# Window attention, forward and backward: the attention products recast as 64x64 tiles

## The chip, the cores and the metric

The kernel runs on one core of a Trainium2 chip. The metric is the device time of one execution in microseconds; the median of seven runs before the change is 1990.57 us (1983.88 to 1993.39). The profile is of one further execution.

## The reference, cut to what matters

An image of 256x256 positions with 384 channels is cut into 1024 windows of 8x8 positions (64 tokens). Each window gets single-head attention without bias; the kernel must return the output and, for a given gradient of the output, the gradients of `x`, `wqkv` and `wo`.

```python
xw = windows of x                     # (1024, 64, 384)
q, k, v = split(xw @ wqkv)            # 384 -> 3 * 384
p = softmax((q @ k.T) * 384 ** -0.5)
out_0 = unwindow((p @ v) @ wo)
out_1, out_2, out_3 = vjp(grad_out)   # of x, wqkv, wo
```

All tensors are bf16.

## The kernel before

**Algebra.** The weights are multiplied together once at the start. With A = Wq Wk^T (scaled), B = Wv Wo and their transposes, a window with tokens x and output gradient g needs: y = x A and z = g B^T (`project`), scores y x^T and dP = z x^T (`scores`), u = x B and v = x A^T (`uv`), softmax P and its gradient dS (`soft`), and then in `attend` three kinds of result: the output o = P u; the gradient d = P^T z + dS^T y + dS v; and U = dS x and W = P^T g, out of which the weight gradients are summed over all windows (`gf_group`, GF_acc). The left factor of a matmul is its stationary operand and is taken transposed, so P and dS as they stand serve P^T z, P^T g and dS^T y, and the turned ones (`PS`) serve P u, dS v and dS x.

**Tiling.** Two windows (128 tokens) are a tile, four tiles a quad; there are 128 quads. Tokens lie on the 128 partitions, window 0 of a tile on the lower half (LO) and window 1 on the upper (HI). z and y leave `project` with channels on the partitions, as columns (window, token) of one tile `yz` whose four slots are ordered z, y, y, z, and must be turned to tokens on the partitions (`tok`) before `attend` uses them.

**Stages.** `step(c, b, a, ahead)` works on three quads at once: `project` for quad a, `scores`, `soft` and `uv` for quad b, `attend` for quad c, in two pairs of tiles. A quad is loaded (`load`) three steps ahead. `load_turn`, ahead of the step, turns a later quad's dq and xq (dT, xT). In a step the order on TensorE is: `scores`; `uv` (8 banks); `project` kind 0 (z, reads dT); one block of the filler; `attend` of tiles 0 and 1; `project` kind 1 (y, reads xT); another block of the filler; `attend` of tiles 2 and 3. The filler is `gf_group`: 12 matmuls over three earlier quads into one bank, which DVE then adds to GF_acc.

**Order.** The order is written out by hand for all five engines (`manual_schedule`); each engine works its list through in order and waits on semaphores. All products go to one ring of eight PSUM banks, given out in turn: the ninth bank asked for is the first again, and waits until its last reader is done. ACT and DVE copy the banks out: ACT z, y, u, v, o, d and one U, DVE the other U and W and GF_acc. SyncE's queue issues, in this order, dT, xT, PS, four xq loads and tok; GpSimd's the dq loads and the stores.

**Shapes on TensorE.** `split` makes `product` issue a 128x128 product as two of 128 rows and 64 columns. It is set between the two `attend`s, so that `project` kind 1 and the filler there have the 128x64 shape that `attend` begins and ends with (`token_part`). `token_part` (lines 261 to 264) is P^T z + dS^T y of a window in one product of 128 rows: `ps` holds P of one window and dS of it on the two halves, so that the token rows z and y add up over the 128 partitions. It needs dS on the half opposite to P (line 224), and tok with z and y of a window on the two halves. The four products of a window pair in `both` (64x64) go to the four quarters of the array: two straight ones (LO to LO, HI to HI) and two crossed ones (LO to HI, HI to LO). The crossed results land on the other half, so that o and d are each kept in two banks, and a bank holds halves of both tiles; they are stored in one store of 128 rows and two of 64 (lines 292 to 297).

Of the kernel before, what the change touches and what calls it, by code (L numbers as in the profile page):

```python
# [14 lines left out]
P = 128  # L15
# [7 lines left out]
def kernel(  # L23
# [120 lines left out]
    ALL = False  # L144
    split = [ALL]

    def product(out, lhsT, rhs, start, stop):
        if split[0]:
            for h in (LO, HI):
                nc.tensor.matmul(out[h], lhsT=lhsT[:, h], rhs=rhs, start=start, stop=stop)  # L150
        else:
            nc.tensor.matmul(out, lhsT=lhsT, rhs=rhs, start=start, stop=stop)  # L152
# [3 lines left out]
    def project(st, kind, mo):  # L156
        if kind == 0 and mo == 0:
            st["yz"] = qp.tile([P, CK, QUAD, 4, WT], BF16, tag="yz", name="yz")
# [10 lines left out]

    def to_tokens(st):  # L170
        st["tok"] = tok = qp.tile([P, CK, QUAD, 2, P], BF16, tag="tok", name="tok", bufs=3)
        nc.sync.dma_start_transpose(out=tok[:].rearrange("p m t b k -> p (m t b) k"),
                                    in_=st["yz"][:].rearrange("p m t s k -> p (m t s k)"))
# [13 lines left out]
    def soft(st, step):  # L187
# [31 lines left out]
        else:  # L219
# [3 lines left out]
            for w, h, o in ((0, LO, HI), (1, HI, LO)):  # L223
                nc.vector.tensor_tensor(out=ps[o, :, w, :], in0=st["pr"][h, :, :], in1=pd[h, :, :], op=ALU.subtract)

    def uv(st, t, part):
        if t == 0 and part == 0:
            for n in ("uq", "vq"):
                st[n] = qp.tile([P, QUAD, C], BF16, tag=n, name=n)
        wgt, dst, cp = ((B_sb, st["uq"], ENG[EV["u"][t]]), (AT_sb, st["vq"], ENG[EV["v"][t]]))[part]  # L230
        pj = ring.tile([P, C], F32, tag="r")
        for m in range(CK):
            product(pj[:], st["xT"][:, t, m, :], wgt[:, m, :], m == 0, m == CK - 1)
        cp(out=dst[:, t, :], in_=pj[:])  # L234
# [6 lines left out]
    def turned(st, n, t, h):  # L241
        if n in ("PT", "ST"):
            return st["PS"][h, t, int((n == "ST") == (h == LO)), :]
        return st[n][h, t, :]

    def attend(st, pair):
# [7 lines left out]
        def both(straight, crossed, t, outer, **flags):  # L254
            for h, o, (dst, lhs, rhs), fl in ((LO, LO, straight, {}), (LO, HI, crossed, flags), (HI, LO, crossed, flags),
                                              (HI, HI, straight, {})):
                at = dst if dst is not crossed[0] else dst[outer if h == LO else 1 - outer]
                nc.tensor.matmul(at[o, :], lhsT=turned(st, lhs, t, h), rhs=st[rhs][h, t, :],  # L258
                                 **{"start": True, "stop": True, **fl})

        def token_part(t, pd, outer, **flags):
            for w, o in ((0, HI), (1, LO)):
                nc.tensor.matmul(pd[outer if w == 0 else 1 - outer][o, :], lhsT=st["ps"][:, t, w, :],  # L263
                                 rhs=st["tok"][:, :, t, w, :], **flags)

        def keep(name, dst, src):
            for outer in (0, 1):
                sb = ob.tile([P, C], BF16, tag=name, name=name)
                nc.scalar.copy(out=sb[:], in_=src[outer][:])  # L269
                stores.append((dst, sb, outer))  # L270

        t0, t1 = pair
        stores = []
        pu = [bank("pu")]
        po = [bank("po") for outer in (0, 1)]
        pd = [bank("pd") for outer in (0, 1)]
        token_part(t0, pd, 1, start=True, stop=False)
        both((pu[0], "ST", "xq"), (po, "PT", "uq"), t0, 1)
# [47 lines left out]
    def step(c, b, a, ahead):  # L326
# [30 lines left out]
        for mo in range(CK):  # L357
            A(project, 1, mo)
# [120 lines left out]
```

## Time and profile before

| | |
|---|---|
| median of 7 runs | 1990.57 us |
| profiled execution | 1990.69 us, its span 1988.9 us |
| TensorE busy | 1967.2 us, 19487 matmuls |
| VectorE (DVE) busy | 1260.2 us |
| ScalarE (ACT) busy | 1461.2 us |
| GpSimd (POOL) busy | 1122.7 us, DMA issues |
| DMA | 423.66 MB, mean 213 GB/s |
| granted TensorE clock | 1.000 |
| issue to landing, median | tok 8.2, xT 6.7, dT 6.6, PS 4.8 us |

A group line of the profile names the source line, engine, operation, the tiles written and read, the shape and count; behind the first bar busy time and mean duration (ns), behind the second the idle time of the engine just before it and what ended it. In the order of time a line has the start, the duration (both us), the engine and how many instructions are merged. Matmul durations overlap: what one costs is the distance from its start to the next one's. "128*64" is the part of the array that a product uses, rows by columns. SPq is SyncE's queue.

### The profile page before, as it was taken

The page shows a single profiled execution, that of the slowest core. Times are in us where ns is not written, and L with a number is a line of the kernel's source. Part 1 is how long each engine was busy: PE and PEld are TensorE (multiplying, and loading weights), DVE is VectorE, ACT ScalarE, POOL GpSimd, SP SyncE. Part 2 cuts the span into 40 slices and gives each one's busy share as a digit, 9 for nine tenths or more (in the row PEclk, how much of TensorE's full clock was granted, in tenths as well). Part 3 has the DMA queues.
Part 4 walks back from the last instruction along what each step waited for, and adds up shares of the span by engine and source line. Part 5 has one row for each costly group of instructions (what it writes and reads, how often), then busy time and mean ns, then how long its engine had stood idle before and what let it go on. Part 6 is the DMA issues. An engine that isn't in the chain of part 4 may idle for free.

```text
span 1988.9 us, 52531 instructions
## 1 busy us (share of the span) xinstructions
PE 1967.2 (99%) x19487; PEld 1125.2 (57%) x19487; DVE 1260.2 (63%) x2860; ACT 1461.2 (73%) x3357; POOL 1122.7 (56%) x2054
## 2 busy tenths in 40 slices
PE   9999999999999999999999999999999999999999
PEld 5555555555555555555555555555555555555555
DVE  5656666666666666666666666666666666666666
ACT  7867777777777777777777777777777777777774
POOL 3655555555555556555555565555555655655553
PEclk9999999999999999999999999999999999999999
DMA  8999999999999999999999999999999999999994
GB/s 178 222 205 219 208 227 208 219 219 214 219 216 219 223 206 228 216 208 217 219 218 214 222 210 221 213 221 218 226 216 219 213 216 213 222 221 220 210 210 108
DMA packets 1036032, 423.66 MB, mean 213 GB/s; under 512 B 918016, under 2 KB 1011200, under 8 KB 1035776
## 3 DMA queue, kind: packets, MB, share of 16 engines
q1 hardware_dynamic: 935984, 267.85, 81.3%
q0 software_dynamic: 98304, 151.39, 30.8%
q8 instruction: 152, 2.49, 0.5%
q10 hardware_dynamic: 1488, 1.08, 0.2%
q14 instruction: 104, 0.85, 0.2%
HBM read 101.84 MB, written 101.84 MB: 102 GB/s over the span
## 4 chain that ended last, share of the span: by engine, by line
PE 82%; DMA 4%; ACT 1%; DVE 0%; SPq 0%; issue 0%; ACTq 0%
PE pj L152 30%; PE pg L152 11%; PE pj L150 11%; PE pg L150 11%; PE pd L263 6%; PE pu L258 5%; PE sd L152 4%; PE pw L258 4%; DMA dT<-dq 3%; DMA PS<-ps 1%; PE pd L258 0%; PE pe L377 0%; ACT uq L234 0%; ACT vq L234 0%; SPq L134 0%
## 5 line engine op out<-in xcount | busy, mean ns | idle before, releaser
L297 POOL DMA_DIRECT2D out_dram<-o x256 | 139.1, 543 | 682.6 <-ACT o L269 663.4
L313 DVE TENSOR_TENSOR GF_acc<-pg,GF_acc 128x384 f32<-128x384 f32 x258 | 143.9, 558 | 527.3 <-PE pg L150 372.3
L269 ACT CAST o<-po 128x384 bf16<-128x384 f32 x512 | 221.8, 487 | 248.0 <-issue 247.7
L152 PEld LDWEIGHTS <-xT 128*128 128x128 bf16 x3072 | 291.9, 98 | 182.3
L152 PE MATMUL pj<-B_sb,xT 128*128 128x384 bf16 x1536 | 333.4, 326 | 0.0
L152 PE MATMUL pj<-AT_sb,xT 128*128 128x384 bf16 x1536 | 333.3, 326 | 0.0
L127 POOL DMA_DIRECT2D dq<-in_grad_out_dram x512 | 274.2, 546 | 82.7 <-DMA out_dram<-o 42.9
L152 PE MATMUL pj<-dT,BT_sb 128*128 128x512 bf16 x1152 | 269.7, 379 | 10.5 <-DMA dT<-dq 7.5
L150 PE MATMUL pj<-xT,A_sb 128*64 128x512 bf16 x2304 | 270.2, 379 | 0.0
L234 ACT CAST uq<-pj 128x384 bf16<-128x384 f32 x512 | 247.6, 484 | 29.3 <-PE pj L152 25.2
L234 ACT CAST vq<-pj 128x384 bf16<-128x384 f32 x512 | 249.8, 488 | 2.1
L269 ACT CAST d<-pd 128x384 bf16<-128x384 f32 x512 | 227.1, 510 | 0.2 <-ACT o L269 0.2
L152 PEld LDWEIGHTS <-xq 128*128 128x128 bf16 x1572 | 153.6, 98 | 114.7 <-issue 0.3
L150 PEld LDWEIGHTS <-xq 128*64 128x64 bf16 x3000 | 167.8, 110 | 89.0
L212 ACT COPY ps<-Pb 64x256 bf16<-64x256 bf16 x256 | 103.3, 403 | 149.7 <-DVE Pb L209 148.2
L168 ACT CAST yz<-pj 128x512 bf16<-128x512 f32 x384 | 208.0, 655 | 0.3 <-PE pj L150 0.2
L166 ACT CAST yz<-pj 128x512 bf16<-128x512 f32 x384 | 206.3, 639 | 0.6 <-PE pj L152 0.2
L152 PEld LDWEIGHTS <-BT_sb 128*128 128x128 bf16 x1152 | 111.4, 98 | 136.5 <-DMA dT<-dq 16.5
L150 PEld LDWEIGHTS <-A_sb 128*64 128x64 bf16 x2304 | 131.5, 110 | 97.5 <-DVE D L218 0.4
L152 PE MATMUL pg<-Uq,xq 128*128 128x384 bf16 x1032 | 181.6, 326 | 0.0
L258 PE MATMUL pu<-xq,PS 64*64 64x384 bf16 x1024 | 175.6, 335 | 2.5 <-DMA PS<-ps 2.0
L263 PE MATMUL pd<-tok,ps 128*64 128x384 bf16 x1024 | 177.6, 344 | 0.0
(87 smaller groups left out, 3388.0 us busy)
## 6 DMA issues: line engine op xcount, KB each, us to landing
xq<-in_x_dram SPq DMA_DIRECT2D x512, 96.0 KB, 4.1
dq<-in_grad_out_dram POOLq DMA_DIRECT2D x512, 96.0 KB, 4.0
out_dram<-o POOLq DMA_DIRECT2D x256, 96.0 KB, 4.3
out_dram<-o POOLq DMA_DIRECT2D x512, 48.0 KB, 4.4
out_dram<-d POOLq DMA_DIRECT2D x256, 96.0 KB, 4.6
out_dram<-d POOLq DMA_DIRECT2D x512, 48.0 KB, 4.6
tok<-yz SPq DMA_TRANSPOSE x128, 8.2
PS<-ps SPq DMA_TRANSPOSE x128, 4.8
```

What stands on the lines that cost most here:

```text
L127: nc.gpsimd.dma_start(out=dq[:, t, :], in_=windows(grad_out, st, 2 * t))
L150: nc.tensor.matmul(out[h], lhsT=lhsT[:, h], rhs=rhs, start=start, stop=stop)
L152: nc.tensor.matmul(out, lhsT=lhsT, rhs=rhs, start=start, stop=stop)
L166: ENG[EV["z"][mo]](out=yz[:, mo, :, 0:4:3, :], in_=pj[:])
L168: ENG[EV["y"][mo]](out=yz[:, mo, :, 1:3, :], in_=pj[:])
L212: nc.scalar.copy(out=ps[h, :, w, :], in_=Pb[h, :, :])
L234: cp(out=dst[:, t, :], in_=pj[:])
L258: nc.tensor.matmul(at[o, :], lhsT=turned(st, lhs, t, h), rhs=st[rhs][h, t, :], **{"start": True, "stop": True, **fl})
L263: nc.tensor.matmul(pd[outer if w == 0 else 1 - outer][o, :], lhsT=st["ps"][:, t, w, :], rhs=st["tok"][:, :, t, w, :], **flags)
L269: nc.scalar.copy(out=sb[:], in_=src[outer][:])
L297: nc.gpsimd.dma_start(out=windows(dst, st, 2 * t0 + 1), in_=sb[:])
L313: nc.vector.tensor_tensor(out=GF_acc[:, f, ma, :], in0=pw[:], in1=GF_acc[:, f, ma, :], op=ALU.add)
```

## The change

- z and y are no longer turned out of `yz`: DVE first copies them apart into a new tile `zy` (`gather`, once for z after the first `attend`, once for y after `project` kind 1), and `tok` is turned out of `zy`, z and y in two blocks, window 0 on LO and window 1 on HI. `yz` has one buffer instead of two.
- DVE also keeps dS on the half where it is computed (`dS`); the crossed copy in `ps` stays, for the turn.
- `token_part` goes. P^T z and dS^T y are 64x64 products. In `attend` each pair of tiles has six groups (`slot`) of four 64x64 products: two straight ones, into a bank of W, U or o, and two crossed ones that add to d (P^T z, dS^T y, dS v). o is now straight: a bank of o holds one tile, and is stored in one store of 128 rows. A crossed sum of d gets all its terms from the same half.
- `split` goes: `project` kind 1 and the filler are 128x128 everywhere.
- `uv` makes u and v of a tile alternately, with two banks at once, and copies both out after that.
- The first W of each pair is copied by ACT; all U and the second W by DVE. POOL issues five stores per pair instead of six.

```diff
--- before.py
+++ after.py
@@ -141,21 +141,14 @@
                 nc.tensor.transpose(pt[:, m, :], st[src][:, t, m * P:(m + 1) * P], ident[:])
             copy_out(t, st[dst][:, t, :, :], pt[:])
 
-    ALL = False
-    split = [ALL]
-
     def product(out, lhsT, rhs, start, stop):
-        if split[0]:
-            for h in (LO, HI):
-                nc.tensor.matmul(out[h], lhsT=lhsT[:, h], rhs=rhs, start=start, stop=stop)
-        else:
-            nc.tensor.matmul(out, lhsT=lhsT, rhs=rhs, start=start, stop=stop)
+        nc.tensor.matmul(out, lhsT=lhsT, rhs=rhs, start=start, stop=stop)
 
     ENG = {"D": nc.vector.tensor_copy, "A": nc.scalar.copy}
 
     def project(st, kind, mo):
         if kind == 0 and mo == 0:
-            st["yz"] = qp.tile([P, CK, QUAD, 4, WT], BF16, tag="yz", name="yz")
+            st["yz"] = qp.tile([P, CK, QUAD, 4, WT], BF16, tag="yz", name="yz", bufs=1)
         yz = st["yz"]
         wgt, src = ((BT_sb, st["dT"]), (A_sb, st["xT"]))[kind]
         pj = ring.tile([P, QUAD, 2, WT], F32, tag="r")
@@ -167,10 +160,16 @@
         else:
             ENG[EV["y"][mo]](out=yz[:, mo, :, 1:3, :], in_=pj[:])
 
+    def gather(st, kind):
+        if kind == 0:
+            st["zy"] = qp.tile([P, 2, CK, QUAD, 2, WT], BF16, tag="zy", name="zy")
+        src = st["yz"][:, :, :, 0:4:3, :] if kind == 0 else st["yz"][:, :, :, 1:3, :]
+        nc.vector.tensor_copy(out=st["zy"][:, kind, :, :, :, :], in_=src)
+
     def to_tokens(st):
-        st["tok"] = tok = qp.tile([P, CK, QUAD, 2, P], BF16, tag="tok", name="tok", bufs=3)
-        nc.sync.dma_start_transpose(out=tok[:].rearrange("p m t b k -> p (m t b) k"),
-                                    in_=st["yz"][:].rearrange("p m t s k -> p (m t s k)"))
+        st["tok"] = tok = qp.tile([P, 2, CK, QUAD, P], BF16, tag="tok", name="tok", bufs=3)
+        nc.sync.dma_start_transpose(out=tok[:].rearrange("p b m t k -> p (b m t) k"),
+                                    in_=st["zy"][:].rearrange("p b m t s k -> p (b m t s k)"))
 
     def scores(st):
         yz, xT = st["yz"], st["xT"]
@@ -222,25 +221,31 @@
             ps = st["ps"]
             for w, h, o in ((0, LO, HI), (1, HI, LO)):
                 nc.vector.tensor_tensor(out=ps[o, :, w, :], in0=st["pr"][h, :, :], in1=pd[h, :, :], op=ALU.subtract)
-
-    def uv(st, t, part):
-        if t == 0 and part == 0:
+            st["dS"] = dS = qp.tile([P, QUAD, WT], BF16, tag="dS", name="dS")
+            nc.vector.tensor_tensor(out=dS[:], in0=st["pr"][:], in1=pd[:], op=ALU.subtract)
+
+    def uv(st, t):
+        if t == 0:
             for n in ("uq", "vq"):
                 st[n] = qp.tile([P, QUAD, C], BF16, tag=n, name=n)
-        wgt, dst, cp = ((B_sb, st["uq"], ENG[EV["u"][t]]), (AT_sb, st["vq"], ENG[EV["v"][t]]))[part]
-        pj = ring.tile([P, C], F32, tag="r")
+        parts = [(wgt, dst, cp, ring.tile([P, C], F32, tag="r", name="pj"))
+                 for wgt, dst, cp in ((B_sb, st["uq"], ENG[EV["u"][t]]), (AT_sb, st["vq"], ENG[EV["v"][t]]))]
         for m in range(CK):
-            product(pj[:], st["xT"][:, t, m, :], wgt[:, m, :], m == 0, m == CK - 1)
-        cp(out=dst[:, t, :], in_=pj[:])
+            for wgt, dst, cp, pj in parts:
+                product(pj[:], st["xT"][:, t, m, :], wgt[:, m, :], m == 0, m == CK - 1)
+        for wgt, dst, cp, pj in parts:
+            cp(out=dst[:, t, :], in_=pj[:])
 
     def turn(st):
         st["PS"] = dst = qp.tile([P, QUAD, 2, WT], BF16, tag="PS", name="PS")
         nc.sync.dma_start_transpose(out=dst[:].rearrange("p t s k -> p t (s k)"),
                                     in_=st["ps"][:].rearrange("p t w k -> p (t w k)"))
 
-    def turned(st, n, t, h):
+    def operand(st, n, t, h):
         if n in ("PT", "ST"):
             return st["PS"][h, t, int((n == "ST") == (h == LO)), :]
+        if n in ("z", "y"):
+            return st["tok"][h, int(n == "y"), :, t, :]
         return st[n][h, t, :]
 
     def attend(st, pair):
@@ -251,50 +256,47 @@
         def bank(name):
             return ring.tile([P, C], F32, tag="r", name=name)
 
-        def both(straight, crossed, t, outer, **flags):
-            for h, o, (dst, lhs, rhs), fl in ((LO, LO, straight, {}), (LO, HI, crossed, flags), (HI, LO, crossed, flags),
-                                              (HI, HI, straight, {})):
-                at = dst if dst is not crossed[0] else dst[outer if h == LO else 1 - outer]
-                nc.tensor.matmul(at[o, :], lhsT=turned(st, lhs, t, h), rhs=st[rhs][h, t, :],
-                                 **{"start": True, "stop": True, **fl})
-
-        def token_part(t, pd, outer, **flags):
-            for w, o in ((0, HI), (1, LO)):
-                nc.tensor.matmul(pd[outer if w == 0 else 1 - outer][o, :], lhsT=st["ps"][:, t, w, :],
-                                 rhs=st["tok"][:, :, t, w, :], **flags)
-
-        def keep(name, dst, src):
-            for outer in (0, 1):
-                sb = ob.tile([P, C], BF16, tag=name, name=name)
-                nc.scalar.copy(out=sb[:], in_=src[outer][:])
-                stores.append((dst, sb, outer))
+        def slot(straight, crossed, start=False, stop=False):
+            for h in (LO, HI):
+                dst, lhs, rhs, t = straight
+                products = [(h, dst[h, :], lhs, rhs, t, {"start": True, "stop": True})]
+                lhs, rhs, t = crossed
+                o = OTHER[h.start]
+                dst = pd[int((t == t0) == (h == LO))]
+                products.append((o, dst[o, :], lhs, rhs, t, {"start": start, "stop": stop}))
+                for o, dst, lhs, rhs, t, flags in products if h == LO else products[::-1]:
+                    nc.tensor.matmul(dst, lhsT=operand(st, lhs, t, h), rhs=operand(st, rhs, t, h), **flags)
+
+        def keep(name, src):
+            sb = ob.tile([P, C], BF16, tag=name, name=name)
+            nc.scalar.copy(out=sb[:], in_=src[:])
+            return sb
 
         t0, t1 = pair
-        stores = []
-        pu = [bank("pu")]
-        po = [bank("po") for outer in (0, 1)]
+        pw = {t: bank("pw") for t in pair}
+        pu = {t0: bank("pu")}
         pd = [bank("pd") for outer in (0, 1)]
-        token_part(t0, pd, 1, start=True, stop=False)
-        both((pu[0], "ST", "xq"), (po, "PT", "uq"), t0, 1)
-        (nc.vector.tensor_copy if t0 else nc.scalar.copy)(out=st["Uq"][:, t0, :], in_=pu[0][:])
-        pw = [bank("pw")]
-        both((pw[0], "Pb", "dq"), (pd, "ST", "vq"), t0, 1, start=False, stop=True)
-        nc.vector.tensor_copy(out=st["Wq"][:, t0, :], in_=pw[0][:])
-        pu.append(bank("pu"))
-        both((pu[1], "ST", "xq"), (po, "PT", "uq"), t1, 0)
-        keep("o", out_0, po)
-        nc.vector.tensor_copy(out=st["Uq"][:, t1, :], in_=pu[1][:])
-        pw.append(bank("pw"))
-        both((pw[1], "Pb", "dq"), (pd, "ST", "vq"), t1, 0, start=True, stop=False)
-        nc.vector.tensor_copy(out=st["Wq"][:, t1, :], in_=pw[1][:])
-        token_part(t1, pd, 0, start=False, stop=True)
-        keep("d", out_1, pd)
-        for dst, sb, outer in stores:
-            if outer:
-                nc.gpsimd.dma_start(out=windows(dst, st, 2 * t1 + 1, 1), in_=sb[LO, :])
-                nc.gpsimd.dma_start(out=windows(dst, st, 2 * t0, 1), in_=sb[HI, :])
-            else:
-                nc.gpsimd.dma_start(out=windows(dst, st, 2 * t0 + 1), in_=sb[:])
+        po = {t0: bank("po")}
+        pu[t1] = bank("pu")
+        po[t1] = bank("po")
+        slot((pw[t0], "Pb", "dq", t0), ("Pb", "z", t0), start=True)
+        nc.scalar.copy(out=st["Wq"][:, t0, :], in_=pw[t0][:])
+        slot((pw[t1], "Pb", "dq", t1), ("dS", "y", t0))
+        nc.vector.tensor_copy(out=st["Wq"][:, t1, :], in_=pw[t1][:])
+        slot((pu[t0], "ST", "xq", t0), ("Pb", "z", t1), start=True)
+        nc.vector.tensor_copy(out=st["Uq"][:, t0, :], in_=pu[t0][:])
+        slot((po[t0], "PT", "uq", t0), ("dS", "y", t1))
+        o0 = keep("o", po[t0])
+        slot((pu[t1], "ST", "xq", t1), ("ST", "vq", t0), stop=True)
+        nc.vector.tensor_copy(out=st["Uq"][:, t1, :], in_=pu[t1][:])
+        slot((po[t1], "PT", "uq", t1), ("ST", "vq", t1), stop=True)
+        o1 = keep("o", po[t1])
+        d = [keep("d", pd[outer]) for outer in (0, 1)]
+        nc.gpsimd.dma_start(out=windows(out_0, st, 2 * t0), in_=o0[:])
+        nc.gpsimd.dma_start(out=windows(out_0, st, 2 * t1), in_=o1[:])
+        nc.gpsimd.dma_start(out=windows(out_1, st, 2 * t0 + 1), in_=d[0][:])
+        nc.gpsimd.dma_start(out=windows(out_1, st, 2 * t1 + 1, 1), in_=d[1][LO, :])
+        nc.gpsimd.dma_start(out=windows(out_1, st, 2 * t0, 1), in_=d[1][HI, :])
 
     fill = []
 
@@ -333,17 +335,13 @@
         B(soft, 0)
         if b is not None and c is None:
             weight_rest()
-        B(uv, 0, 0)
-        B(uv, 0, 1)
+        B(uv, 0)
         B(soft, 1)
-        B(uv, 1, 0)
-        B(uv, 1, 1)
+        B(uv, 1)
         B(soft, 2)
         B(soft, 3)
-        B(uv, 2, 0)
-        B(uv, 2, 1)
-        B(uv, 3, 0)
-        B(uv, 3, 1)
+        B(uv, 2)
+        B(uv, 3)
         B(soft, 4)
         for mo in range(CK):
             A(project, 0, mo)
@@ -353,12 +351,12 @@
             load(ahead)
         filler(1)
         C_(attend, (0, 1))
-        split[0] = True
+        A(gather, 0)
         for mo in range(CK):
             A(project, 1, mo)
+        A(gather, 1)
         A(to_tokens)
         filler(1)
-        split[0] = ALL
         C_(attend, (2, 3))
 
     G_ON_PE, X_ON_PE = 4, 1
@@ -443,7 +441,6 @@
             elif len(held) == GQ:
                 fill.append(gf_group(held))
                 held = []
-        split[0] = False
         filler(1 << 30)
         weight_gradients(last)
 
```

## The prediction

> **What bounds the kernel now.** I read the page's totals first, then the order of time on TensorE over one step, then the same on SyncE's queue.
>
> ```profile
> PE 1967.2 (99%) x19487; PEld 1125.2 (57%) x19487; DVE 1260.2 (63%) x2860; ACT 1461.2 (73%) x3357; POOL 1122.7 (56%) x2054
> DMA  8999999999999999999999999999999999999994
> PE 82%; DMA 4%; ACT 1%; DVE 0%; SPq 0%; issue 0%; ACTq 0%
> L152 PE MATMUL pj<-dT,BT_sb 128*128 128x512 bf16 x1152 | 269.7, 379 | 10.5 <-DMA dT<-dq 7.5 <-ACT vq L234 1.9 <-ACT ps L212 1.0
> ```
>
> TensorE hardly stops, and where it does, it waits for the DMA transpose of dq. But the sixteen DMA engines are at nine tenths in every slice too. So two resources stand close together, and the question is how far apart. TensorE from one `scores` to the next (start, duration, both us):
>
> ```profile
> 1004.93 0.87 PE L152 MATMUL sd<-xT,yz 128*128 128x64 bf16 x24
> ...
> 1018.67 0.33 PE L263 MATMUL pd<-tok,ps 128*64 128x384 bf16 x2
> 1018.93 0.35 PE L258 MATMUL pu<-xq,PS 64*64 64x384 bf16 x1
> ...
> 1019.11 0.32 PE L258 MATMUL pw<-dq,Pb 64*64 64x384 bf16 x1
> ...
> 1019.27 0.32 PE L258 MATMUL pu<-xq,PS 64*64 64x384 bf16 x1
> ...
> 1019.49 0.32 PE L258 MATMUL pw<-dq,Pb 64*64 64x384 bf16 x1
> ...
> 1019.78 0.35 PE L263 MATMUL pd<-tok,ps 128*64 128x384 bf16 x2
> 1020.06 0.87 PE L152 MATMUL sd<-xT,yz 128*128 128x64 bf16 x24
> ```
>
> A step is 20.06 - 4.93 = 15.13 us, and 105 of the 127 step distances in the trace have this length; 18 longer ones add 15.3 us in all (mean of all 15.19). Between the lines the starts are what counts, because matmuls overlap. A group of four 64x64 products costs 0.16 us when its neighbour is another such group, as does a pair of 128x64 products among its own kind. Where the shape changes it costs 0.26 (into 64x64), 0.29 (out of it) and 0.28 (from 128x64 to 128x128).
>
> SyncE's queue in the same step:
>
> ```profile
> 1007.26 1.21 SPq L238 DMA_TRANSPOSE PS<-ps  x1
> 1008.52 2.83 SPq L126 DMA_DIRECT2D xq<-in_x_dram  x4
> 1011.46 4.67 SPq L172 DMA_TRANSPOSE tok<-yz  x1
> 1016.35 2.28 SPq L134 DMA_TRANSPOSE dT<-dq  x1
> 1018.80 3.19 SPq L134 DMA_TRANSPOSE xT<-xq  x1
> 1022.15 1.30 SPq L238 DMA_TRANSPOSE PS<-ps  x1
> ```
>
> One ends where the next begins: 14.28 of 15.13 us are inside issuing instructions, the rest is gaps of some 0.05 us. And it is late. The PS issued at 1007.26 belongs to the step before, whose `ps` was ready about ten us earlier. The dT issued at 1016.35 is needed by `project` kind 0 at 1009.54 + 15.13 = 1024.67; with the median 6.6 us to landing it comes at 1022.9, so 1.7 us in hand (over all steps I find 0 to 3.6, median 1.7). That margin is the distance of the two resources.
>
> [...] +0.10 to +0.13 us at each change above. [...] So waits would stand as gaps in SyncE's list; there are none, and SyncE runs at its own pace. [...]
>
> **The change, part by part** (per step, two pairs).
>
> TensorE in `attend`. Before, a pair is 2 pairs of 128x64 and 4 groups of 64x64. From the starts, the first pair takes 1.24 us (1013.53 to 1014.77), the second 1.39 plus 0.09 on entering it from 128x128 in the first: 2.73 us per step. After, it is 6 groups of four 64x64 products. The streaming is the same (6 x 0.1625 = 0.975 us); only the shape changes differ. Six groups: 0.19 for the first distance (median in the trace), 4 x 0.163, then 0.28 out: 1.12 us; going in costs 0.26 - 0.16 = 0.10 more. So 1.22 us per pair, 2.44 per step: **0.29 us less**. A direct change between 128x128 and 64x64 isn't in the trace; 0.24 to 0.33 covers it if it costs 0.02 more or less than its neighbours each time.
>
> `project` kind 1 and the filler as whole 128x128 products: 18 products in 2.11 us become 9 in 2.11 us (kind 0 has that form: also 2.11). Nothing won; 1628 fewer matmuls in all, counting the 1024 more in `attend`.
>
> u and v interleaved: the same 24 products of 0.1625. The u bank is full 0.49 us later. ACT then copies uq and vq of tile 1 together, 0.87 us instead of one in time, so `exp` starts about 0.37 us later, and with it `pr`, the last reader of the `sd` bank that the first filler needs. `pr` ends at 1010.73 and the filler starts at 1011.49: 0.76 us of cover, 0.4 left. Cost nothing; without cover up to 0.4 us a step.
>
> Wq of t0 goes to ACT in both pairs (before: Uq, first pair only): ACT +0.48, DVE -0.55. The new dS costs DVE 0.43 (as `pd`, 425 ns). ACT rises to 11.8 of 15.1 us, no bound.
>
> The two gathers. These stand in DVE's queue between the casts of the first pair and the second filler's sum, where DVE is idle now:
>
> ```profile
> 1015.32 0.55 DVE L289 CAST Wq<-pw 128x384 bf16<-128x384 f32 x1
> 1018.88 0.56 DVE L313 TENSOR_TENSOR GF_acc<-pg,GF_acc 128x384 f32<-128x384 f32 x1 [3.01 <-PE pg L150]
> ```
>
> The second waits for ACT's last y copy, which ends at 1017.70 (1.62 us from 1016.08), so there are 1.15 us before GF_acc is due at 1018.88. [...] Queued behind it are GF_acc (its bank is the last `po` of the next `attend`) and the Wq and Uq casts, whose banks the next `uv` takes.
>
> Queues. SyncE's orders are the same in number and size: tok is 24 blocks from zy instead of yz, and now follows the gather[...]. SyncE reaches tok some 9 us after y is ready, so this wait isn't seen; nor is that of the next dT and xT behind it. If SyncE caught up, they'd each come that much later. POOL issues 10 stores a step instead of 12, the same bytes: one order of 0.56 us less per pair on a queue with time to spare. yz in one buffer: z of the next step is copied after `scores` and the gathers, some 6 us before. Nothing.
>
> **The sum.** Were TensorE alone the bound, 128 x 0.29 = 37 us would go: 1990.7 - 37 = 1954. But with steps of 14.84 TensorE uses up the 1.7 us margin on dT in six steps. From then on the step is SyncE's. Its pace, from dT issue to dT issue, has a mean of 15.23 us from the eighth interval on, but it isn't fixed: in the 13 intervals that began over 12.5 us into the step (SyncE behind) it was 14.85. It has also kept to 15.13 over stretches of some 20 steps without a stall, so it gives way to TensorE's phase, presumably by what the stores take from the engines. I take the middle of 14.85 and 15.23, 15.04, less the work of two small stores: 15.03. That is 15.19 - 15.03 = 0.16 us in 127 steps, 20 us, and 1 us in the last steps, which have no dT: **1969 us** against the profiled execution's 1990.69 (span 1988.9 and 1.8 around it). The median of the seven runs is 1990.57, so no correction.
>
> **Rivals.** A is the forecast: part of the gain is eaten by waits for dT, 1960 to 1984. For it: SyncE is never idle and late.
>
> B: the transposes follow TensorE as they did at 15.13; steps of 14.84 with as many long ones as now: **1954**, 1947 to 1960. For it: no drift in long stretches; 14.85 when behind. Against: hiccups of 2 us, one in seven to twenty steps, hit a smaller margin.
>
> C: SyncE's pace stays 15.2 whatever TensorE does, the gain is all waits for dT: **1990**, 1984 to 1994.6. For it: the mean of 15.23, engines at nine tenths. Against: the 14.85.
>
> D: slower. [...] GF_acc is 0.5 us late and releases the last `po` bank about 0.35 us after its group is due, in every step. With waits for dT on top 15.3 us a step: **2003**, 1995 to 2015. It begins to cost at 1.15 us, eats the whole 0.29 at about 1.6. For it: [...] the later `exp` takes cover from the same banks. [...]
>
> **Chances.** A 0.40, B 0.25, C 0.19, D 0.16. Some 0.2% (4 us) is what a measurement of this kernel can tell from no change. C lies half within it, the rest of C splits to the faster side: faster 0.70, same 0.14, slower 0.16. The range leaves out D and the fast end of B: 1949 to 1994; A's own is 1960 to 1984.
>
> **What would show it.** Right: six even starts 0.16 us apart in `attend`, one change into and one out of 64x64 per pair, `attend` at 2.44 us a step; idle time before `pj<-dT` growing from 10 us to some 20 to 35; steps of unequal length with 14.84 as the shortest[...]. Wrong: waits on TensorE for ACT or DVE (banks), groups 0.2 us apart or more, a gather over 1.15 us, or SyncE with gaps before tok. B would be shown by idle time before dT as now; C by nearly every step being stalled on dT, some 40 us in all.

## The result, and the profile after

The changed kernel takes 1948.46 us (median of 12 runs, 1942.39 to 1956.82) beside 1989.96 us for the kernel before (median of 31 runs): a ratio of 0.979, with a 95% interval of 0.977 to 0.981. One further run, of the kernel with swapped stores below, had a granted clock of 0.851 and took 2204.75 us; it is left out of every figure. The forecast was 1969 us with 1949 to 1994 around it. The sign was right; the time lies 0.5 us beyond the fast end of the range, and the gain is twice the one forecast. Of the four cases it is B, the transposes following TensorE; the likeliest one, A, did not come.

The profiled execution took 1949.48 us, its span 1947.7. The totals, the DMA row of the slices, the chain that ended last, and two of the costliest groups of the changed kernel:

```profile
PE 1926.2 (99%) x17859; PEld 1079.0 (55%) x17859; DVE 1380.1 (71%) x3116; ACT 1503.2 (77%) x3485; POOL 1006.3 (52%) x1798
DMA  8999999999999999999999999999999999999994
PE 93%; DMA 3%; ACT 2%; DVE 1%; issue 0%; SPq 0%; ACTq 0%
L167 DVE COPY zy<-yz 128x1536 bf16<-128x1536 bf16 x256 | 147.3, 576 | 192.4 <-ACT yz L161 190.0
L145 PE MATMUL pj<-dT,BT_sb 128*128 128x512 bf16 x1152 | 269.7, 379 | 5.1 <-DMA dT<-dq 1.9
```

TensorE is as full as before, with less to do. The wait in front of `project` kind 0 that was to grow from 10 us to some 20 to 35 has shrunk to 5. TensorE's list of waits (what waited, for what, us in total, times, longest) has these two put down to DMA:

```profile
PE pu L268 <- DMA PS<-ps: 6.6, 5, 2.3
PE pj L145 <- DMA dT<-dq: 1.9, 3, 1.5
```

Two more in front of `project` kind 0, of 1.71 and 1.25 us, are put down to ACT there; but in both the dT had landed 46 or 47 ns before TensorE went on, as in the three above, so they were waits for dT too: 4.9 us in five. (Of the 10.5 us of the kernel before, 10.4 were waits for dT by the same count.)

One step in the order of time on TensorE (start, duration, both us):

```profile
1011.66 0.87 PE L145 MATMUL sd<-xT,yz 128*128 128x64 bf16 x24
...
1023.32 2.11 PE L145 MATMUL pg<-Uq,xq 128*128 128x384 bf16 x12
1025.36 0.35 PE L268 MATMUL pw<-dq,Pb 64*64 64x384 bf16 x1
...
1025.55 0.33 PE L268 MATMUL pd<-tok,dS 64*64 64x384 bf16 x2
...
1025.71 0.32 PE L268 MATMUL pu<-xq,PS 64*64 64x384 bf16 x1
...
1026.20 0.33 PE L268 MATMUL pd<-vq,PS 64*64 64x384 bf16 x2
...
1026.46 0.61 PE L145 MATMUL sd<-xT,yz 128*128 128x64 bf16 x15
```

A step is 14.796 us in the median (before 15.129). The distances between the six groups of `attend` are 0.187, 0.162, 0.163, 0.162 and 0.163 us, and 0.265 us out: 1.102 us. The way in shows as a filler of 2.043 instead of 1.950 us, 0.093 more. That is 1.195 us per pair, 2.39 per step, where 2.73 stood.

SyncE's queue in the same stretch:

```profile
1002.34 4.42 SPq L171 DMA_TRANSPOSE tok<-zy  x1
1006.99 1.47 SPq L134 DMA_TRANSPOSE dT<-dq  x1
1008.63 3.17 SPq L134 DMA_TRANSPOSE xT<-xq  x1
1011.97 1.82 SPq L241 DMA_TRANSPOSE PS<-ps  x1
1013.85 3.30 SPq L126 DMA_DIRECT2D xq<-in_x_dram  x4
1017.25 4.46 SPq L171 DMA_TRANSPOSE tok<-zy  x1
```

It is still one order against the next, with gaps of 0.05 to 0.25 us (some 0.5 ahead of xT in one step of eight), and still late: tok starts a median of 7.5 us after its gather is ready, and dT lands 2.3 us ahead of its use (before 1.7). The same 24 blocks, the same bytes: only the durations are shorter. tok is 4.63 us in the mean instead of 4.90. The queue seldom held TensorE up; it ran faster.

The sum of the change in the trace: 127 steps at 0.333 us less are 42.3 us. Three short steps at the start (12.4 to 12.9 us), which have no filler, gain nothing (1.4 us less than that), and the steps longer than the median by over 0.1 us add 15.3 us, much as before (15.1 by the same count). That leaves some 41 us; measured are 40.9 between the first and the last `scores`, and 41.2 between the profiled executions. In two further traces of the changed kernel the long steps add 10.9 and 11.9 us instead of 15.3. They are not all chance: the 86th step is long in all three, and in two of a nearly equal kernel (u and v apart, below), for a reason that I do not know.

### The profile page after: what moved, and what is told of

Read it like the earlier page. It is cut to its first block, busy times and chain, and to the rows that moved or that the text cites. A ratio compares the mean times of both kernels' runs of the same rounds, so it can differ in the third digit from the quotient of the medians.

```text
span 1947.7 us, 48767 instructions
## 1 busy us (share of the span) xinstructions
PE 1926.2 (99%) x17859; PEld 1079.0 (55%) x17859; DVE 1380.1 (71%) x3116; ACT 1503.2 (77%) x3485; POOL 1006.3 (52%) x1798
## 3 DMA queue, kind: packets, MB, share of 16 engines
q1 hardware_dynamic: 935984, 267.85, 79.4%
q0 software_dynamic: 86016, 151.24, 31.1%
## 4 chain that ended last, share of the span: by engine, by line
PE 93%; DMA 3%; ACT 2%; DVE 1%; issue 0%; SPq 0%; ACTq 0%
PE pj L145 49%; PE pg L145 25%; PE pw L268 5%; PE sd L145 5%; PE pu L268 4%; PE po L268 4%; DMA PS<-ps 2%; DMA dT<-dq 1%; PE pd L268 1%; ACT vq L237 0%; DMA xq<-in_x_dram 0%; ACT uq L237 0%; ACT yz L161 0%; ACT yz L159 0%; PE pe L375 0%
## 5 line engine op out<-in xcount | busy, mean ns | idle before, releaser
L145 PE MATMUL pj<-B_sb,xT 128*128 128x384 bf16 x1536 | 499.5, 327 | 0.0
L145 PE MATMUL pj<-AT_sb,xT 128*128 128x384 bf16 x1536 | 499.4, 326 | 0.0
L145 PEld LDWEIGHTS <-xq 128*128 128x128 bf16 x3072 | 300.1, 98 | 225.8 <-issue 1.4
L167 DVE COPY zy<-yz 128x1536 bf16<-128x1536 bf16 x256 | 147.3, 576 | 192.4 <-ACT yz L161 190.0
L283 ACT CAST Wq<-pw 128x384 bf16<-128x384 f32 x256 | 123.3, 482 | 195.4 <-PE pw L268 195.4
L145 PE MATMUL pg<-Uq,xq 128*128 128x384 bf16 x1536 | 270.4, 326 | 0.5 <-DVE GF_acc L315 0.5
L145 PE MATMUL pj<-xT,A_sb 128*128 128x512 bf16 x1152 | 270.9, 381 | 0.0
L145 PE MATMUL pg<-Wq,xq 128*128 128x384 bf16 x1536 | 270.4, 326 | 0.0
L272 ACT CAST o<-po 128x384 bf16<-128x384 f32 x512 | 221.3, 485 | 10.4 <-PE po L268 7.8
L299 POOL DMA_DIRECT2D out_dram<-d x256 | 178.6, 697 | 15.7 <-issue 7.6
```

The source lines that it names most:

```text
L167: nc.vector.tensor_copy(out=st["zy"][:, kind, :, :, :, :], in_=src)
L272: nc.scalar.copy(out=sb[:], in_=src[:])
L283: nc.scalar.copy(out=st["Wq"][:, t0, :], in_=pw[t0][:])
L299: nc.gpsimd.dma_start(out=windows(out_1, st, 2 * t0, 1), in_=d[1][HI, :])
```

## The experiments

"Alone" times are a single execution with its profile. Twelve runs of the changed kernel lie between 1942 and 1957 us, so that some 10 us between two single executions say nothing by themselves; the steps in the traces say more. Four short notions recur: the **lead** of a dT is the time from its landing to its first use; the **pace** is the mean distance from one dT issue on SyncE to the next; a **late** queue reaches tok many us after its gather; TensorE's **own step** is the shortest common one, without waits. All four are worked out from the traces.

### Was TensorE the bound before?

The split shape is taken out of the kernel before, nothing else. It adds two changes of shape to each step, and no DMA.

```diff
--- before.py
+++ e5
-        split[0] = True
         for mo in range(CK):
             A(project, 1, mo)
```

> The kernel before with 128x128 products everywhere outside the attention (project kind 1 and the filler no longer in two column halves), so two more changes of array shape per step: 0.10 us out of 128x64 and 0.09 us back in. If a step of the kernel before is TensorE's (15.13 us), +0.19 us per step: 2010 to 2018. If it is the transposes' pace, as the forecast had it for what came after: 1988 to 1996.

1999.97 us alone beside 1992.66 for the kernel before. The step went from 15.129 to 15.280, the mean pace of SyncE with it (15.23 to 15.29, counted from the eighth interval on as in the prediction), and dT's lead rose from 1.7 to 2.7 us. So the kernel before was bound by TensorE, a cost on TensorE alone comes through, and the queue without gaps makes room for it. The time lies between the two that were expected: of 0.15 x 127 = 19 us some 10.6 came back, because the steps longer than the median by over 0.1 us add only 4.6 us here, and 15.1 before. The two changes cost 0.15 us together rather than 0.19: the 64x64 part of the second pair fell from 0.85 to 0.77 us.

### How fast are the transposes by themselves?

Two runs take work from TensorE, one adds work to the queue, all in the changed kernel. The first leaves the filler sums out (the weight gradients are then incomplete), the second two of the twelve products of each filler block; the third transposes PS a second time, into a tile that nobody reads.

```diff
--- after.py
+++ e1
-                fill.append(gf_group(held))
+++ e6
         n = len(sts) * QUAD
         for f in range(2):
...
+                if not last:
+                    n = 10
+++ e3
+        again = qp.tile([P, QUAD, 2, WT], BF16, tag="PS2", name="PS2", bufs=1)
+        nc.sync.dma_start_transpose(out=again[:].rearrange("p t s k -> p t (s k)"),
+                                    in_=st["ps"][:].rearrange("p t w k -> p (t w k)"))
```

> Leaves out the weight-gradient sums (the filler) of all quads but the last ones, so that a step costs TensorE about 14.80 - 2 x 2.0 = 10.8 us while the DMA traffic per step stays. Theory of the forecast (SyncE's chain of transposes has a pace of its own of 14.85 to 15.2 us): steps of 14.9 or more, time 1930 to 1960, every step stalled on dT or PS. Rival 1 (the chain yields to TensorE and has much to spare): steps of 12 to 13.5, time 1580 to 1770. Rival 2 (its own pace is just under 14.8): steps of 14.3 to 14.8, time 1870 to 1920.

> The changed kernel with the last two of twelve products of each filler block left out (the weight gradients lack them): TensorE 0.65 us less per step, 14.15. Theory K1 (the transposes have an own pace of about 14.85 to 15.1 which the changed kernel has just reached): 1940 to 1960, waits for dT and PS in most steps. Theory K2 (they follow TensorE down): 1866 to 1885.

> PS is transposed a second time into a tile that nobody reads: 1.6 us of issue per step more on SyncE's queue and 8% more transposed blocks. Forecast and rival 2 (the queue has less than 0.3 us to spare per step): steps of 15.9 to 16.4, time 2090 to 2150. Rival 1 (much to spare): steps stay near 14.8, time under 1965.

Without the filler, 1958.51 us alone, no less than the changed kernel, though 3024 products are gone, some 490 us of TensorE's work (an estimate, at 0.1625 us each). Its waits:

```profile
PE pu L268 <- DMA PS<-ps: 186.3, 92, 4.8
PE pj L145 <- DMA dT<-dq: 104.3, 60, 4.7
```

The pace is then 15.1 us, and the shortest common step 12.90 us (not 10.8 as I expected; its waits for ACT in `attend` are only 5.0 us in five, and what the rest of the difference is was not shown). With ten products per block, 1948.26 us alone, the time of the changed kernel: TensorE's own step fell to 14.373, and what it saved came back as waits.

```profile
PE pu L268 <- DMA PS<-ps: 44.9, 41, 3.0
PE pj L145 <- DMA dT<-dq: 10.8, 13, 2.4
```

The mean step is 14.87 between the first and last `scores`, as in the changed kernel.

Waiting has a second price here, which my sums leave out. One of these waits, of 3.01 us, ends at 317.85 us. Two stretches around it (from and to, length, TensorE's busy time and products, its granted clock; the last two figures are of the DMA engines) show the clock at 0.50 for 6.8 us, from 0.95 us before that end on:

```profile
306.04:316.90 10.86, 8.79 (x79) 1.00 1.15 183
316.90:323.72 6.82, 5.88 (x27) 0.50 1.16 240
```

In this run five such stretches, of 3.4 or 6.8 us, begin within 3.5 us of the start of a wait of 2.1 to 3.0 us. Without the filler there are 53, 215 us in all, and the mean clock is 0.945; the changed kernel, whose longest wait is 2.3 us, has none before its end.

With PS twice, 2141.11 us alone, the pace is 16.48; the added order takes 1.46 us of it up to the next one's start, and 15.02 is left. Its waits:

```profile
PE pu L271 <- DMA PS<-ps: 84.0, 68, 4.1
PE pj L145 <- DMA dT<-dq: 53.5, 51, 3.8
```

So there is a floor under the mean step, about 14.87 us in this form of the kernel. The changed kernel, whose steps with the long ones come to 14.87 in the mean (14.84 in two further traces), stands close to it, and the further cut of 0.42 us on TensorE was worth nothing. The floor is neither sharp nor one number, though. 105 of the changed kernel's 127 steps have TensorE's own 14.796 us, and in one stretch of 44 steps without a wait for DMA the pace was 14.78. And it is 15.0 with the second transpose and 15.1 without the filler.

### SyncE's issuing or the DMA engines?

First the xq loads go to GpSimd's queue, in the kernel without filler, so that SyncE issues some 2.5 us less per step (four orders of 0.63):

```diff
--- e1
+++ e8
-            nc.sync.dma_start(out=xq[:, t, :], in_=windows(x, st, 2 * t))
+            nc.gpsimd.dma_start(out=xq[:, t, :], in_=windows(x, st, 2 * t))
```

> As the run without the filler (steps of 15.1 us, 1958), and the four xq loads of a step issued from GpSimd's queue instead of SyncE's: 2.8 us of issue less per step on SyncE, the same traffic. If SyncE's issuing sets the pace: 15.1 - 2.8 = 12.3 us per step, 1590 to 1700. If the sixteen DMA engines set it: 14.8 to 15.2, 1925 to 1965.

2019.55 us alone, outside both forecasts: the pace went from 15.1 to 15.67 us, and tok's issue from 4.4 to 6.5 us in the mean. But the run moves more than SyncE's issuing. The xq loads now stand between the dq loads in GpSimd's queue, and dq comes late: a dT starts a median of 0.14 us after the last of its dq loads has landed, where it was 17.7 us without this edit. So SyncE stands idle ahead of dT, 2.0 us in the mean instead of 0.2:

```profile
1015.03 7.47 SPq L171 DMA_TRANSPOSE tok<-zy  x1
1023.79 2.77 SPq L134 DMA_TRANSPOSE dT<-dq  x1
```

This run therefore doesn't tell what sets the pace in the others. The next two do.

Then the traffic: the stores of out_0 and out_1 are left out from the third quad on (those outputs stay unwritten), with all filler products and with ten.

```diff
--- after.py
+++ e2 (with e6's edit as well: e11)
+        if st["i"] >= 2:
+            return
         nc.gpsimd.dma_start(out=windows(out_0, st, 2 * t0), in_=o0[:])
```

> Leaves out the stores of both large outputs after the second quad; everything else stays. If the stores are what holds SyncE's queue about half a step late (rival 1), the queue catches up with TensorE: gaps before tok and PS, dT landed 8 us or more ahead of its use, no long steps, time about 1949 - 11 = 1938. If the queue's lateness is its own pace (forecast, rival 2), dT stays 0 to 4 us ahead and the time stays at 1945 to 1950.

> Ten of twelve products per filler block (TensorE 14.37 us per step at least) and no stores after the second quad. Theory K1 (with all traffic the sixteen DMA engines need about 14.85 us a step, and TensorE at 14.37 waits for them): without the stores' traffic the steps fall to 14.37 and the time to 1937 - 127 x 0.43 = 1883 (1876 to 1890). If something else holds the run with ten products at 1948, it stays at 1930 or more.

1936.98 and 1881.66 us alone. In both TensorE keeps its own step throughout (14.796 and 14.373), with no wait for a transpose; the floor is gone. SyncE in the first of them, where it has caught up:

```profile
1004.83 3.66 SPq L171 DMA_TRANSPOSE tok<-zy  x1
1008.72 2.35 SPq L134 DMA_TRANSPOSE dT<-dq  x1
1011.24 2.83 SPq L134 DMA_TRANSPOSE xT<-xq  x1
1014.37 1.19 SPq L241 DMA_TRANSPOSE PS<-ps  x1
1015.61 2.50 SPq L126 DMA_DIRECT2D xq<-in_x_dram  x4
1019.63 3.67 SPq L171 DMA_TRANSPOSE tok<-zy  x1
```

Between 1018.11 and 1019.63 it waits for the gather: a gap, at last. tok takes 3.68 us (4.63 with the stores), dT's lead is 11.3 us, and 12.3 of 14.8 us are inside orders. The floor goes with the stores. They are not on SyncE's queue, so its own issuing is not what sets the floor; what the two share, as far as the traces show, are the sixteen DMA engines (170 instead of 220 GB/s over the slices without the stores; the packets of the queue with GpSimd's transfers took 10.9% of the engines' span there and 31.1% with the stores, those of SyncE's 77.3 and 79.4%). And a queue without gaps can be one whose orders are being stretched.

### Why does the queue stay late?

With a floor of 14.87, a queue beside steps of 15.13 should make up a quarter of a us each step and be ready on time after some forty. In the kernel before it never was. Two runs slow TensorE alone: the first product of each filler block is done again two or four times and counted once.

```diff
--- after.py
+++ e15 (-2) and e14 (-4)
-                for i in range(n):
+                for j in range(0 if last else -2, n):
+                    i = max(j, 0)
                     st, t = sts[i // QUAD], i % QUAD
-                    product(..., i == 0, i == n - 1)
+                    product(..., j <= 0, j < 0 or j == n - 1)
```

> The changed kernel with two products more in each filler block (the first one of the block done three times, its result counted once): two blocks a step, so TensorE's own step is 14.80 + 4 x 0.1625 = 15.45 us. Theory F (the DMA engines have an own pace of about 14.87 us a step, whatever TensorE does): with 0.58 us in hand per step the queue makes up its lateness of about 11 us in some 20 steps, and after that dT lands about 10 us ahead of its use as in the kernel without stores; steps 15.45 without long ones, 2026 to 2034 us. Theory G (the pace gives way to TensorE's phase: the queue stays one step late): dT stays 2 to 4 us ahead over the whole run, the issues stretch to fill the 15.45 us; about the same time, 2028 to 2040 us, with a few long steps. The time hardly tells them apart, the lateness does.

> The same with four products more in each filler block: TensorE's own step is 14.80 + 8 x 0.1625 = 16.10 us. Theory F: 1.2 us in hand per step, the queue has caught up after some 10 steps, dT then lands about 10 us or more ahead, 2108 to 2116 us. Theory G: dT stays a few us ahead as in the kernel without the extra products; 2108 to 2122 us. If 15.45 stays late and 16.10 catches up, the pace reaches up to a limit between the two, and then the 14.87 is the pace only for a queue that stands behind.

2017.9 and 2098.71 us alone, some 10 us below what I expected, because the long steps are all but gone (2 with 1.9 us in all, and none). With own steps of 15.447 us, the queue stays late: tok 6.6 us after its gather, dT's lead 3.7 us (1.6 to 5.7 in eight of ten), no gaps beyond those of the changed kernel, tok stretched to 5.05 us in the mean. With 16.096 it catches up in some twenty steps: tok starts when the gather ends, with a gap of 1.1 us ahead of it, dT's lead is 10.9 us, and 13.9 of 16.1 us are inside orders. A dT and its use, first at 15.447 (SyncE, then TensorE):

```profile
1008.99 2.22 SPq L134 DMA_TRANSPOSE dT<-dq  x1
...
1019.11 2.11 PE L145 MATMUL pj<-dT,BT_sb 128*128 128x512 bf16 x9
```

and at 16.096:

```profile
1008.40 2.57 SPq L134 DMA_TRANSPOSE dT<-dq  x1
...
1026.79 2.10 PE L145 MATMUL pj<-dT,BT_sb 128*128 128x512 bf16 x9
```

The first dT lands at 1015.42, the second at 1016.52: 3.7 and 10.3 us ahead. So a late queue goes along with TensorE's rate, from 14.80 up to 15.45 us at least, and keeps its lateness. A mean pace read off such a queue is TensorE's, not its own. Neither theory held over the whole stretch; the third outcome that the expectation named did.

What sets the rate of a late queue is then likely to be something tied to TensorE's step, and the stores are. The first try to move them:

```diff
--- after.py
+++ e10
-        nc.gpsimd.dma_start(out=windows(out_0, st, 2 * t0), in_=o0[:])
...
+        st.setdefault("kept", []).append((t0, t1, o0, o1, d))
+        if pair[0] == 0:
+            return
+        for t0, t1, o0, o1, d in st["kept"]:
+            nc.gpsimd.dma_start(out=windows(out_0, st, 2 * t0), in_=o0[:])
...
```

> The changed kernel with the five stores of the first pair of a step issued only after the second pair, right before its own: the same traffic, but all ten stores of a step in one burst after the second attention, none under the dT transpose. If the position of the store bursts is what holds SyncE's queue in its place behind TensorE: dT lands clearly earlier or later than now (median 2.4 us ahead of its use), by 1.5 us or more, and the long steps change with it (time 1938 to 1945, or 1955 to 1975). If not: dT 1.5 to 3 us ahead, 1943 to 1955.

1946.2 us alone, and it says nothing on the question: GpSimd issues nothing of its own between the two pairs' stores, so its list came out in the order that it had, and in the trace the stores stand where they stood. It is one more run of the changed kernel. The second try puts the second pair's five stores first, so that the first pair's wait behind them:

```diff
--- e10
+++ e16
-        for t0, t1, o0, o1, d in st["kept"]:
+        for t0, t1, o0, o1, d in reversed(st["kept"]):
```

> The changed kernel with the five stores of each step's first pair held until after the five of its second pair, in GpSimd's own order of issues: all ten then stand in one run that begins where the second pair's outputs are ready, about the start of the next step, instead of 0.6 to 3.3 and 10.3 to 12.9 us into it; the four dq loads come behind them, some 3 us later. Nothing else moves, the traffic is the same. Theory S (what decides the pace of SyncE's queue is which of its transfers the stores meet; in the changed kernel the first pair's meet tok): tok's issue gets shorter than 4.3 us, dT lands 5 us or more ahead of its use, no waits for DMA are left: 1936 to 1944 us. Theory T (the amount of traffic alone decides): dT's lead stays 1 to 4 us, 1943 to 1952 us. If the one run of ten is worse than two of five, the lead falls below 1 us and it takes over 1955 us.

2017.03 us (median of three runs); against the kernel before a ratio of 1.016 (1.012 to 1.020), and some 70 us slower than the changed kernel with the same traffic. GpSimd's queue in it, one run of ten orders:

```profile
1021.13 0.55 POOL L299 DMA_DIRECT2D out_dram<-o  x1 [5.96 <-ACT o L272]
...
1025.55 0.58 POOL L302 DMA_DIRECT2D out_dram<-d  x1
1027.07 0.57 POOL L303 DMA_DIRECT2D out_dram<-d  x1 [0.94 <-DMA out_dram<-d]
1029.02 1.09 POOL L127 DMA_DIRECT2D dq<-in_grad_out_dram  x2 [1.37 <-issue]
```

and in the changed kernel, two runs of five:

```profile
1021.93 0.54 POOL L295 DMA_DIRECT2D out_dram<-o  x1 [4.24 <-ACT o L272]
...
1024.10 0.87 POOL L299 DMA_DIRECT2D out_dram<-d  x1
1027.03 0.54 POOL L295 DMA_DIRECT2D out_dram<-o  x1 [2.06 <-ACT o L272]
```

The pace went from 14.90 to 15.47 us a step, dT's lead fell to 0.6 us, and TensorE waits:

```profile
PE pj L145 <- DMA dT<-dq: 37.9, 28, 3.9
PE pu L268 <- DMA PS<-ps: 20.9, 23, 2.2
```

The amount of traffic alone is not what decides: where the stores stand in the step moved the pace by over 0.5 us. (The dq loads moved with them, by some 3 us; no dT waited for its dq, which had landed 5.2 us or more before.) That was theory S in kind, but its direction was wrong; the third outcome that the expectation named came. I had the first pair's stores down as the harmful ones because they meet tok; taking them away from it and putting them in one run with the others made it worse. What stays open is which meeting costs, and by what the rate of a late queue locks to TensorE. Only that the place of GpSimd's transfers, the stores above all, matters is shown.

### The gather

The copy of y is done three times, the last of which counts, to see what a late gather would have done.

```diff
--- after.py
+++ e9
-        nc.vector.tensor_copy(out=st["zy"][:, kind, :, :, :, :], in_=src)
+        for again in range(3 if kind else 1):
+            nc.vector.tensor_copy(out=st["zy"][:, kind, :, :, :, :], in_=src)
```

> The y gather three times instead of once (1.12 us more on DVE per step, between the last y copy and the second filler's sum). By the arithmetic of the forecast's slow case (cover of 1.15 us for 1.7 us) GF_acc comes 0.5 us late and the last bank of the attention 0.35 us: steps of 15.1 to 15.2, 1985 to 2000. Rival (DVE's banks have more cover than that): under 1955.

1986.31 us alone, step 15.179: the second `attend` takes 1.486 instead of 1.102 us, 0.385 more. The wait stands where rival D put it:

```profile
PE po L269 <- DVE GF_acc L316: 23.4, 123, 0.2
```

It is a wait of 0.19 us, 123 times; the rest of the 0.385 shows only as longer distances between the starts of the groups, since matmuls overlap. So D's mechanism is real, with 0.35 us forecast for it, and it stayed away because one gather takes 0.56 us.

### u and v

The interleaving of u and v is undone in the changed kernel; later it and the changed kernel were timed side by side, five runs each.

```diff
--- after.py
+++ e4, e12
-        for m in range(CK):
-            for wgt, dst, cp, pj in parts:
-                product(pj[:], ...)
-        for wgt, dst, cp, pj in parts:
-            cp(out=dst[:, t, :], in_=pj[:])
+        for m in range(CK):
+            product(pj[:], ...)
+        cp(out=dst[:, t, :], in_=pj[:])
...
-        B(uv, 0)
+        B(uv, 0, 0)
+        B(uv, 0, 1)
```

> The changed kernel with u and v made one after the other again, as before. If interleaving costs nothing and brings nothing (forecast): 1945 to 1952, ratio to the kernel before 0.977 to 0.981. If exp's 0.37 us delay counts, this version is faster by up to 10 us; if two banks at once help, slower.

> u and v one after the other in the changed kernel, now in five rounds beside the changed kernel itself. If it is really better (exp and so PS earlier): 2 to 6 us below the changed kernel. If the first difference (1944.2 against 1948.5) was scatter: within 2 us of it.

> The changed kernel itself, five rounds, as the partner of the run before: 1945 to 1952, ratio to the kernel before 0.977 to 0.981.

1944.24 us (ratio 0.978, 0.975 to 0.980) at first; 1943.22 (0.977, 0.975 to 0.980) beside 1946.38 (0.979, 0.977 to 0.982) for the changed kernel side by side. The own step is 14.796 either way. The first four steps are 0.2 us shorter each with u and v apart; the rest of the difference is in the long steps (10.4 and 9.6 us of excess beside 10.9 to 15.3 in three traces of the changed kernel), which vary from run to run. So the interleaving brings nothing, and the version without it was 3 to 4 us ahead both times, though the intervals overlap. It is the fastest that I ran of the kernels that leave nothing out.

## Why the prediction was wrong

**The step that failed** is the pace in the sum: "I take the middle of 14.85 and 15.23, 15.04, less the work of two small stores: 15.03." With it failed the sentence that it serves, "From then on the step is SyncE's": 105 of 127 steps kept TensorE's own 14.796 us, the pace was 14.90, and 14.78 over 44 steps. The 14.85 was near what ten products per block showed (14.87), though no fixed limit either. The 15.23 was no pace of SyncE's own. It was the mean step of the kernel before (15.19, or 15.25 without its first four steps), which TensorE imposed; a queue that goes along with TensorE can't be averaged for its own speed, and the runs at 15.28, 15.45 and 15.18 us show it going along in each. With 14.87 in the sum the same working gives 1990.7 - (15.19 - 14.87) x 127 = 1950 us. The sentence before it had already noted that the queue "gives way to TensorE's phase" for stretches of twenty steps; taking that at its word was rival B.

**What misled** is the reading of the queue without gaps: "there are none, and SyncE runs at its own pace." (There are gaps, of 0.05 to 0.23 us and now and then 0.5, 0.85 us a step in all and not 0.05 each. The shortest of them stand in the runs that keep up as well, so they are no waits.) The runs do show a wait as a gap: 1.1 us ahead of tok at 16.1 us a step and 1.2 without the stores (medians). But the reverse doesn't follow. An order that other traffic holds back is long without any gap: the same tok took 3.58 to 7.16 us within one run (that of the slow gather). No gaps meant late and stretched, not at the limit.

**TensorE's term** had the right mechanism and was undersized: 0.29 us forecast, 0.333 measured, 5.5 us over the run. It stood in rival B's sum and not in the 1969. Six even distances of 0.163, one change in and one out; but the change in cost 0.093 instead of 0.10, the first distance was 0.187 instead of 0.19, and the way out 0.265 instead of 0.28. The trace prices a change of shape at 0.09 to 0.10 us, either way between 128x128 and 64x64 (0.093 more on the way in; 0.265 out, beside 0.163 between groups). Both errors went the same way.

**What held.** The gather took 0.56 us in the median (0.55 to 0.64) and fell into the 1.15 us of cover. That it would fit was an assumption of mine, and so was the 1.7 us that rival D took for it; nothing in the trace of the kernel before showed either. D's place and price were confirmed by making the gather late. The later `exp`, the ACT and DVE loads, `yz` in one buffer and the whole 128x128 products cost nothing on the path: 105 of the changed kernel's steps are not longer than 14.80 for any of them. (In the first four steps, which have no filler as cover, u and v apart are 0.2 us faster.) tok behind the gather wasn't seen, since the queue came 7.5 us after it. A was right that the two resources are close: the floor with ten products per block lies some 0.07 us above the changed kernel's own step (14.87 and 14.80), where A had 0.19 (15.03 and 14.84).

**Of the rivals,** B gave 1954 with long steps as before, and 0.25 chance. With the right size of TensorE's term, 0.333, its working gives 1948; that this is the measured time to 0.5 us is in part luck, since the long steps happened to add the same 15 us as before. C (1990) would have needed a fixed pace; the runs exclude it.

## What to carry to other kernels

A queue that is always busy and always late has no speed that can be read off its mean (15.23 us here, with a floor of some 14.87): find its floor from the fastest intervals, or by taking the other engine's work away in an experiment. Stretched orders (the same transfer at 3.7 us without the stores and 4.6 with them) were the sign here that the queue shares something with other traffic. Leaving that traffic out took the floor away; moving it made things worse, so its place has to be tried, not argued. A run that takes orders off the queue must be looked at for what comes late in the other queue. Before cutting the bound engine further, ask how far below it the next floor lies: here the first 0.33 us per step were worth all they promised, and the next 0.42 nothing. And look at the granted clock of a run that waits: the waits alone are not its whole cost (0.945 in the mean without the filler).

## What the runs showed of the hardware

- A late transpose queue held its lateness over 120 steps beside steps of 15.45 us and let go of it at 16.10, though the same orders fit into 13.9 us there. I know no reason in the traces for two such states.
- In the changed kernel the four 64x64 products of a group of `attend` began within some 0.01 us of one another, and a group cost 0.163 us, as one product of the whole array does (0.1625 in the filler). Each of these products lasted 0.32 to 0.35 us: they overlap.
- Moving ten stores within the step, with no byte more, changed the pace from 14.9 to 15.47 us. Moving the loads from SyncE to GpSimd changed it from 15.1 to 15.67, with dq late in GpSimd's queue.
- TensorE's granted clock fell to a half for 3.4 us or a multiple around waits: 53 times in the run without the filler, five times with ten products per block (each within 3.5 us of the start of a wait), and between the first and the last step not once in the runs without stores or at 16.10 us, where TensorE did not wait.
- GpSimd's last store of a pair took 0.87 us (0.75 to 0.87 in eight of ten) where a gather on DVE ran during it, 118 times, and 0.57 us in the other 138. The first two stores of a pair, beside a gather 126 and 115 times, were only 1 to 6 ns longer. None of TensorE's waits in this trace is for GpSimd.
